# The first batch's last 64 tokens done later for four pairs at once, and q of three pairs loaded in 1 KB runs

## The chip, the cores and the metric

The kernel runs on one core of a Trainium2 chip. The metric is the device time of the whole program in microseconds. The core has a matrix engine (TensorE, "PE" in the profile, with its weight loads as "PEld"), three engines for elementwise work (VectorE "DVE", ScalarE "ACT", GpSimd "POOL"), and a sync engine "SP", which here only issues DMAs. ACT issues DMAs as well.

## The reference

A retention layer without softmax is followed by a SwiGLU feed-forward block. Eight batches, eight heads, 576 tokens, head width 64; then 4608 tokens of width 512 and a hidden width of 1536.

```python
scores = scale * np.matmul(q, k.transpose(0, 1, 3, 2))
gamma = 1.0 - 2.0 ** (-5.0 - np.arange(H, dtype=np.float32))
Dmat = np.where(rel >= 0, gamma[:, None, None] ** rel[None, :, :], 0.0)
ret = scores * Dmat[None, :, :, :]
return np.matmul(ret, v).astype(np.float32)
...
x = np.ascontiguousarray(attn_out.transpose(0, 2, 1, 3)).reshape(B * S, H * D)
...
g = x @ w_gate
silu = g * (1.0 / (1.0 + np.exp(-g)))
val = x @ w_val
return (silu * val @ w_out).astype(np.float32)
```

## The kernel before

Attention works by pairs of heads: pair `i` is batch `i // 4`, heads `2p` and `2p + 1` with `p = i % 4`, and there are 32 pairs. The 576 tokens of a pair are nine chunks of 64. Within a chunk the scores are masked by decay (`near`, with the separate `last_near` for the ninth chunk); what earlier chunks contribute goes through a running 64x64 state for each head. A pair passes through three `tick`s: in tick `i` its q and k are transposed and its k is scaled (`transposes`), in tick `i + 1` come scores, chunk states and masks (`scores`, `new_states`, `masked`), in tick `i + 2` the values and their way into `x` (`own_values`, `earlier_values`, `to_x`). The values of a pair gather in one PSUM tile, `outer`; scores and states use another, `inner`; four more banks, A, B, C and E, belong to the projections and, in the first batch, to the transposes.

The order of the instructions on every engine is written out by hand, and each engine takes its instructions in that order. First come ticks 0 to 5 for the first batch (pairs 0 to 3). During these nothing else can be done, since the feed-forward block needs `x`. The first batch's q and k are loaded token-major and transposed by PE against an identity (L471), copied out of PSUM (L472), and the ninth chunk goes through bankC in the same way (L476, L479). `load(i)` issues the DMAs of pair `i`; in the first batch a row of the load is 64 floats. Batches from the second on are loaded with 32-wide rows and transposed by DVE in 32x32 blocks (L489).

From the moment when the first two pairs are in `x` the up-projection `up0` of the first 512 tokens begins (L772): a 128x512 product for each of 12 hidden blocks `f`, gate and value, into banks A and B for even `f` and C and E for odd. Its weights arrive in DMAs of 256 KB, later of 1 MB (L385, L387), are taken apart by ACT (`split`, L404 and L405) and put together with rounding by DVE (`rounding`, L418 and L419). After the first two `f`, a `plan` is worked off: for each `f` from 2 on the roundings due, `up0(f)`, the next load, and a tick of the second batch: tick 4 after `f=2`, tick 5 after `f=3`, tick 6 after `f=5`. So the PE work of tick 5 (states and scores of pair 4) stands between `f=3` and `f=4`. From 512 tokens on the feed-forward block runs in tiles of 1024 tokens by a fast matrix multiplication scheme with written-out sums (L1003 and L1050), with the remaining ticks spread among the steps.

In the first batch SP's queue holds, in order: the small table, the loads of pairs 0 to 3 (shared with ACT's queue for pairs 0 and 1), the second table, sixteen weight DMAs of 256 KB, load 4, one weight DMA of 1 MB, load 5, load 6 and so on. ACT's queue issues the further 1 MB weight loads as its splits make room. The compiler gives each DMA of these two queues one of eight semaphores, in turn; a DMA waits at its issue until the one that had its semaphore before, eight places earlier, has landed.

Names that the change touches: `CW` is 512 (eight chunks of a pair), `D` and `L` are 64, `NC` is 9, `NFULL` is 4, `HP` is 4, `SQ` is 32; `early[i]` holds the transposed q of pair `i` of the first batch; `even` and `state` hold states; `qry` and `qry_odd` are the decays of the queries with the scale, applied in `to_x` by DVE (L627; L651 for the ninth chunk); `key` those of the keys (L504 on DVE and POOL, L506 on ACT).

Of the kernel before, what the change touches and what calls it, by code (L numbers as in the profile page):

```python
# [22 lines left out]
def tables(gamma, scale, L):  # L23
# [12 lines left out]
    pieces = scale * np.stack(half, axis=2).reshape(2 * L, -1)  # L36
    parts = [twice((g[:, None] ** -at).T), twice((g[:, None] ** (L - at)).T),
             both(g[:, None] ** L), both(g[:, None] ** (2 * L)), pieces, both(scale * g[:, None] ** at),
# [116 lines left out]
def kernel(  # L155
# [32 lines left out]
    nc = tc.nc  # L188
# [65 lines left out]
    io = const.tile([P, 1024], F32, name="io")  # L254

# [8 lines left out]
    def whole(i):  # L264

        return i < needed(2) - 2
# [4 lines left out]
    def load(i):  # L271
# [6 lines left out]
        if i < HP:  # L278
            qk = late[0] if late else ld.tile([P, 2, S // SQ, SQ], F32, tag="qk", name="qk").rearrange("p n j d -> p (n j d)")[:, 0 : NC * D]
            queues = (nc.sync, nc.scalar if i < 2 else nc.sync)  # L280
            for dst, src in ((qk, q), (kn, k)):
                dst = dst.rearrange("p (g d) -> p g d", d=D)
                for n, at in enumerate((slice(0, NFULL + 1), slice(NFULL + 1, NC))):
                    queues[n].dma_start(out=dst[:, n::2], in_=tokens(src, b, p)[:, at])
            queues[i % 2].dma_start(out=t.rearrange("p (g d) -> p g d", d=D), in_=tokens(v, b, p))
# [21 lines left out]
    def chunk(i, hl, c, paired=False):  # L307

        if whole(i):
            g, r = divmod(NC * hl + c, 2)  # L310
            g = 2 * g % NC if paired else g
            return half[r], slice(g * D, (g + 1) * D)
        if c + 1 == NC:
            return half[hl], slice(CW, CW + D)
        return half[c % 2], slice((2 * (c // 2) + hl) * D, (2 * (c // 2) + hl + 1) * D)

    def column(i, hl, c):

        return ts((c - hl) % NC if i < HP else c, L)
# [6 lines left out]
    NCOL = 2 * H + 4 * HP  # L326
# [8 lines left out]
    piece = tab[:, NCOL - 2 * HP : NCOL]  # L335
# [12 lines left out]
    decay(slice(0, H), slice(0, H), half[0])  # L348
    decay(odd_heads, even_heads, half[1])
    decay(even_heads, odd_heads, half[1])  # L350
    nc.gpsimd.tensor_copy(out=last_near, in_=near[:, even_heads])
# [71 lines left out]
    for f in range(2):  # L423
        for m in range(2):
# [8 lines left out]
    spare = rest[:, dn_at + 2560 : sum_at]  # L433
    other = (spare[:, 0:CW].rearrange("p (h c i) -> p h c i", h=2, i=L), spare[:, CW : CW + L],
             spare[:, 640 : 640 + NC * D].rearrange("p (c d) -> p c d", d=D))
    early = [spare[:, 640 + S * (1 + i) : 640 + S * (2 + i)] for i in range(HP)]
# [6 lines left out]
    def last_scores(i):  # L443
        return bankE[:, 0:L] if i < HP else sr
# [14 lines left out]
    def transposes(i):  # L459
# [7 lines left out]
        if i < HP:  # L467

            for t, src, bank in ((kT, kn, bankB), (qT, qk, bankA)) if i else ((qT, qk, bankA), (kT, kn, bankB)):
                for c in range(NFULL):  # L470
                    nc.tensor.transpose(bank[:, ts(c, P)], src[:, ts(c, P)], ident)  # L471
                copy(t[:, 0:CW], bank)  # L472
            tails = ((kT, kn), (qT, qk))
            for n, (_, src) in enumerate(tails):
                for hl in range(2):
                    nc.tensor.matmul(bankC[half[hl], ts(n, L)], src[half[hl], CW : CW + D], ident[half[hl], half[hl]],  # L476
                                     start=True, stop=True, skip_group_check=True)
            for n, (t, _) in enumerate(tails):
                copy(t[:, CW:S], bankC[:, ts(n, L)])  # L479
# [13 lines left out]
        def keys():  # L493
            blocks = kn.rearrange("p (g d) -> p g d", d=D)
            if i < HP:
                parts = [(0, every, blocks[:, 0 : NC - 1 : 2]), (1, every, blocks[:, 1:NC:2]), (1, half[1], blocks[half[1], NC - 1])]
            elif whole(i):
# [38 lines left out]
    def new_states(i):  # L536
        s = st[i]
        for c in range(NFULL):
            for r in range(2):
                for hl in range(2):  # L540
                    rows, at = chunk(i, hl, 2 * c + r)
                    nc.tensor.matmul(z[half[hl], r, c], s["kn"][chunk(i, hl, 2 * c + r, i < HP)], s["v"][rows, at],  # L542
                                     start=True, stop=True, skip_group_check=True)

    def earlier_values(i):
# [6 lines left out]
        for hl in range(2):  # L552
# [3 lines left out]
        for c in (1, 3, 4, 6, 5, 7, 2, 8) if whole(i) else range(1, NC):  # L556
            for hl in range(2):
                nc.tensor.matmul(xr[half[hl]] if c + 1 == NC else value(i, hl, c), state[half[hl], c, :],  # L558
                                 s["qT"][half[hl], column(i, hl, c)], start=False, stop=True, skip_group_check=True)
# [656 lines left out]
```

## Time and profile before

| what | us |
|---|---|
| three runs | 1040.08, 1041.9, 1045.64; median 1041.9 |
| the profiled execution | 1040.84 |
| its span (first to last instruction) | 1039.1 |
| PE busy | 1025.6 |
| PE busy in 0 to 40 us | 32.04 |
| DVE busy in 0 to 40 us | 23.92 |
| ACT busy in 0 to 40 us | 16.14 |
| POOL busy in 0 to 40 us | 7.29 |
| first transpose of pair 0 on PE | 4.29 |
| first up-projection on PE | 26.39 |
| PE work of tick 5 begins | 57.81 |

The profile comes from one execution, recorded by the hardware. A row of the timeline reads: start in us, busy us, engine, line, operation, destination and sources, count, and in brackets how long the engine had been idle and what released it. Consecutive instructions of one kind are put together. "SPq" and "ACTq" rows are DMAs at their issue; the time shown is that of the issue, and not of the transfer. Rows of the waits read: engine and line, what it waited for, us in total, times, the longest. Rows of the windows read: the stretch, its length, busy us of each engine with the number of instructions, the granted clock, the busy share of the DMA engines and GB/s. Matmuls are pipelined and their ends are modelled.

### The profile page before, as it was taken

What the parts mean: (1) busy time and instruction counts of PE and PEld (TensorE: products, weight loads), DVE (VectorE), ACT (ScalarE), POOL (GpSimd) and SP (SyncE); (2) the same over time, 40 slices, a digit from 0 to 9 for tenths busy, and PEclk for the clock granted to TensorE, in tenths of its full rate; (3) what the DMA queues carried; (4) which work ended last, traced back from release to release, by engine and by line L of the source; (5) the groups of instructions that cost most, each with busy time, mean ns of one, the idle gap of its engine ahead of it and who ended that gap; (6) DMA issues with size and microseconds to landing.
All of it is one profiled execution on the core that took longest, in us unless ns stands there. A gap on an engine that the chain in (4) does not pass through costs nothing.

```text
span 1039.1 us, 21528 instructions
## 1 busy us (share of the span) xinstructions
PE 1025.6 (99%) x8448; PEld 843.2 (81%) x8448; DVE 642.3 (62%) x1091; ACT 297.4 (29%) x646; POOL 400.5 (39%) x347
## 2 busy tenths in 40 slices
PE   7999999999999999999999999999999999999998
PEld 6444555888888888888888888888888888888887
DVE  5588868776768767546458785435466644344644
ACT  4475433243544222222322103223211022231110
POOL 2002376766565036522133058212240583222505
PEclk9999999999999999999999999999999999999999
DMA  9999877776679887674676686545554465555653
GB/s 244 251 283 276 190 208 270 195 212 191 195 190 256 213 249 217 186 196 134 186 229 173 176 202 216 152 138 153 158 172 150 143 195 154 152 153 162 180 162 100
DMA packets 310380, 199.10 MB, mean 192 GB/s; under 512 B 220168, under 2 KB 254984, under 8 KB 310280
## 3 DMA queue, kind: packets, MB, share of 16 engines
q1 hardware_dynamic: 279000, 161.51, 57.3%
q10 hardware_dynamic: 31280, 36.22, 10.4%
q8 instruction: 67, 1.10, 0.4%
q14 instruction: 33, 0.27, 0.1%
HBM read 157.56 MB, written 40.11 MB: 190 GB/s over the span
## 4 chain that ended last, share of the span: by engine, by line
PE 78%; DVE 2%; issue 1%; ACT 0%; DVEq 0%
PE bankC L1003 13%; PE bankE L1003 13%; PE bankB L1003 13%; PE bankA L1003 13%; PE bankB L1050 6%; PE bankC L1050 6%; PE bankA L1050 6%; PE bankE L1050 6%; PE outer L531 1%; PE inner L572 1%; PE outer L558 1%; PE inner L542 1%; DVE rest L806 1%; DVE arena L806 0%; DVE rest L940 0%
## 5 line engine op out<-in xcount | busy, mean ns | idle before, releaser
L940 POOL TENSOR_TENSOR rest<-rest 128x512 f32<-128x512 f32 x65 | 91.6, 1414 | 299.1 <-DVE rest L940 279.8
L1024 ACT ACTIVATE io<-rest 128x256 f32<-128x256 f32 x180 | 74.8, 416 | 303.5 <-DVE rest L940 260.8
L1003 PE MATMUL bankC<-rest,arena 128*128 128x256 f32 x544 | 129.1, 380 | 0.0
L1003 PE MATMUL bankA<-rest,arena 128*128 128x256 f32 x544 | 128.7, 379 | 0.0
L806 POOL TENSOR_TENSOR arena<-arena 128x512 f32<-128x512 f32 (+1 forms) x72 | 111.5, 1561 | 36.1 <-DMA up<-arena 23.9
L1003 PE MATMUL bankE<-rest,arena 128*128 128x256 f32 x512 | 121.4, 380 | 0.9 <-DVE rest L940 0.9
L1003 PE MATMUL bankB<-rest,arena 128*128 128x256 f32 x512 | 121.2, 379 | 0.0
L1031 POOL TENSOR_TENSOR arena<-rest,io 128x256 f32<-128x256 f32 x72 | 51.9, 726 | 167.8 <-ACT io L1024 167.8
L1003 PEld LDWEIGHTS bankA<-rest,arena 128*128 128x128 f32 x544 | 103.2, 190 | 14.5 <-issue 0.5
L1003 PEld LDWEIGHTS bankC<-rest,arena 128*128 128x128 f32 x544 | 102.9, 190 | 14.6 <-POOL arena L806 0.3
L1003 PEld LDWEIGHTS bankE<-rest,arena 128*128 128x128 f32 x512 | 96.9, 190 | 14.6 <-DVE rest L940 1.4
L1003 PEld LDWEIGHTS bankB<-rest,arena 128*128 128x128 f32 x512 | 97.1, 190 | 13.3
L806 POOL TENSOR_TENSOR rest<-rest 128x256 f32<-128x256 f32 (+1 forms) x66 | 67.4, 1042 | 95.9 <-DMA qk<-in_k_dram 60.1
L940 DVE TENSOR_TENSOR rest<-bankB,rest 128x512 f32<-128x512 f32 x72 | 48.9, 687 | 67.4 <-PE bankB L1003 51.5
L940 DVE TENSOR_TENSOR rest<-bankC,rest 128x512 f32<-128x512 f32 x72 | 48.9, 687 | 65.8 <-PE bankC L1003 47.1
L940 DVE TENSOR_TENSOR rest<-bankA,rest 128x512 f32<-128x512 f32 x72 | 48.9, 687 | 61.5 <-PE bankA L1003 44.1
L940 DVE TENSOR_TENSOR rest<-bankE,rest 128x512 f32<-128x512 f32 x71 | 48.2, 687 | 60.0 <-PE bankE L1003 46.7
L1027 DVE SCALAR_TENSOR_TENSOR arena<-rest,io 128x256 f32<-128x256 f32 x84 | 58.5, 698 | 11.1 <-ACT io L1024 11.0
L1050 PE MATMUL bankB<-arena 128*128 128x256 f32 x252 | 58.3, 381 | 0.3 <-DVE arena L806 0.3
L1050 PE MATMUL bankA<-arena 128*128 128x256 f32 x252 | 58.0, 380 | 0.2 <-DVE arena L806 0.2
L1050 PE MATMUL bankC<-arena 128*128 128x256 f32 x252 | 58.1, 380 | 0.0
L1050 PE MATMUL bankE<-arena 128*128 128x256 f32 x252 | 57.9, 379 | 0.0
(192 smaller groups left out, 1617.0 us busy)
## 6 DMA issues: line engine op xcount, KB each, us to landing
arena<-up SPq DMA_DIRECT2D x234, 256.0 KB, 2.6
arena<-dn SPq DMA_DIRECT2D x104, 384.0 KB, 3.8
up<-arena ACTq DMA_DIRECT2D x78, 256.0 KB, 4.1
dn<-rest SPq DMA_DIRECT2D x78, 128.0 KB, 1.9
out_dram<-rest SPq DMA_DIRECT2D x31, 256.0 KB, 4.1
qk<-in_q_dram SPq DMA_DIRECT2D x108, 72.0 KB, 2.3
qk<-in_k_dram SPq DMA_DIRECT2D x108, 72.0 KB, 3.3
rest<-in_moe_w_out_dram ACTq DMA_DIRECT2D x6, 1024.0 KB, 5.1
```

Of the source, the lines that this page charges most:

```text
L531: m = nc.tensor.matmul(value(i, hl, c), s["v"][rows, at], ret[rows, c % 2 if whole(i) else hl, c // 2], start=start, stop=start, skip_grou ...
L542: nc.tensor.matmul(z[half[hl], r, c], s["kn"][chunk(i, hl, 2 * c + r, i < HP)], s["v"][rows, at], start=True, stop=True, skip_group_check= ...
L558: nc.tensor.matmul(xr[half[hl]] if c + 1 == NC else value(i, hl, c), state[half[hl], c, :], s["qT"][half[hl], column(i, hl, c)], start=Fal ...
L572: nc.tensor.matmul(sc[chunk(i, hl, 2 * c + r)[0], r if whole(i) else hl, c], kT[half[hl], at], qT[half[hl], at], start=True, stop=True, sk ...
L806: eng.tensor_tensor(out=dst, in0=srcs[0], in1=srcs[1], op=ALU.add if op[0] == "add" else ALU.subtract)
L940: eng.tensor_tensor(out=at(op[1]), in0=at(op[2]), in1=at(op[3]), op=ALU.add if op[0] == "add" else ALU.subtract)
L1003: m = nc.tensor.matmul(b[:, gv * TB : (gv + 1) * TB], w[:, gv, ts(c, P)], rhs[:, c, :], start=(opens and gv == 0 and c == 0), stop=(c == 1 ...
L1024: nc.scalar.activation(out=s, in_=src[:, 0:TB], func=AF.Silu, scale=-1.0 if negative else 1.0)
L1027: return lambda: nc.vector.scalar_tensor_tensor(out=dst, in0=src[:, TB : 2 * TB], scalar=-1.0, in1=s, op0=ALU.mult, op1=ALU.mult)
L1031: nc.gpsimd.tensor_tensor(out=dst, in0=src[:, TB : 2 * TB], in1=s, op=ALU.mult)
L1050: nc.tensor.matmul(b[:, m * TB : (m + 1) * TB], lhs[:, qd, ts(m, P)], w[:, qd], start=(opens and qd == 0 and m == 0), stop=(qd == NQ - 1), ...
```

## The change

In the first batch each pair now stops after eight chunks (512 tokens). Its loads are made head by head, k and v still in rows of 64 floats, and q of pairs 1 to 3 in runs of four tokens (1 KB), into the place that the transposed q takes later. GpSimd reads q from there, puts it into the order that the transposes expect, and multiplies it by the decay of the query and the scale (`scale_run`, with the new table `runs`). For these three pairs `to_x` is then a plain copy on ACT, where it was a product on DVE. ACT's copy of the transposed q writes every fourth column. The tail's transposes, copies, scores, values and products of the first batch are gone from ticks 0 to 5.

The last 64 tokens of all four pairs are done in ticks 5 and 6 of the running order, among the up-projections. `end_loads` issues sixteen loads of q and k (128 partitions in all, rows of 32 floats) and four of v on SP, behind load 5 and ahead of load 6. `end_transposes` is two DVE transposes ahead of tick 5. Tick 5 then has `end_scores` on PE behind pair 4's scores, and `end_masks` on DVE; tick 6 has `end_own` and `end_earlier` on PE and `end_to_x` on DVE. The state ahead of the ninth chunk is kept in `end_states`. The change of the decay mask to the layout of the later batches (`decay`, `last_near`) moves behind the first batch. In the fourth pair's tick the first weight split and the transposes change places with the values of pair 1.

```diff
-        return i < needed(2) - 2
+        return HP <= i < needed(2) - 2
+    def scaled(i):
+        return 0 < i < HP
...
-            for dst, src in ((qk, q), (kn, k)):
-                dst = dst.rearrange("p (g d) -> p g d", d=D)
-                for n, at in enumerate((slice(0, NFULL + 1), slice(NFULL + 1, NC))):
-                    queues[n].dma_start(out=dst[:, n::2], in_=tokens(src, b, p)[:, at])
-            queues[i % 2].dma_start(out=t.rearrange("p (g d) -> p g d", d=D), in_=tokens(v, b, p))
+            for h, queue in zip(heads, queues):
+                if scaled(i):
+                    queue.dma_start(out=early[i][:, ts(h % 2, CW // 2)], in_=q[b, h, 0:CW].rearrange("(p c) d -> p (c d)", c=NFULL))
+                else:
+                    queue.dma_start(out=blocks(qk)[:, h % 2], in_=q[b, h, 0:CW].rearrange("(c p) d -> p c d", p=P))
+            for h, queue in zip(heads, queues):
+                queue.dma_start(out=blocks(kn)[:, h % 2], in_=k[b, h, 0:CW].rearrange("(c p) d -> p c d", p=P))
+            for h in heads:
+                queues[i % 2].dma_start(out=blocks(t)[:, h % 2], in_=v[b, h, 0:CW].rearrange("(c p) d -> p c d", p=P))
...
-                copy(t[:, 0:CW], bank)
-            tails = ((kT, kn), (qT, qk))
-            for n, (_, src) in enumerate(tails):
-                for hl in range(2):
-                    nc.tensor.matmul(bankC[half[hl], ts(n, L)], src[half[hl], CW : CW + D], ident[half[hl], half[hl]],
-                                     start=True, stop=True, skip_group_check=True)
-            for n, (t, _) in enumerate(tails):
-                copy(t[:, CW:S], bankC[:, ts(n, L)])
+                if t is qT and scaled(i):
+                    copy(t[:, 0:CW].rearrange("p (t c) -> p c t", c=NFULL), bank.rearrange("p (c t) -> p c t", c=NFULL))
+                else:
+                    copy(t[:, 0:CW], bank)
...
+                    if scaled(i):
+                        nc.scalar.copy(out=dst(lo, end)[to].rearrange("p (c r i) -> p c r i", r=2, i=L)[:, :, r], in_=xo[src, :, r])
+                        continue
...
+    def end_loads():
+        for n, src in enumerate((q, k)):
+            for a in range(P // SQ):
+                for j in range(2):
+                    nc.sync.dma_start(
+                        out=end_raw[a * SQ : (a + 1) * SQ, n].rearrange("t (n j d) -> t n j d", n=HP, d=SQ)[:, :, j],
+                        in_=src[0, a // 2 : H : 2, CW + j * SQ : CW + (j + 1) * SQ, (a % 2) * SQ : (a % 2 + 1) * SQ].rearrange("n t d -> t n d"))
+        for hl in range(2):
+            for x in range(2):
+                nc.sync.dma_start(out=end_v[half[hl ^ x], 2 * x : 2 * x + 2],
+                                  in_=v[0, 4 * x + hl : 4 * x + 4 : 2, CW:S].rearrange("n t d -> t n d"))
+    def end_transposes():
+        for n, to in enumerate((end_q, end_k)):
+            nc.vector.transpose(out=to.rearrange("p n i -> p (n i)"), in_=end_raw[:, n])
+    def end_scores():
+        for n, x, hl in ends:
+            nc.tensor.matmul(end_at[x][half[hl ^ x], n], end_k[half[hl], 2 * x + n], end_q[half[hl], 2 * x + n],
+                             start=True, stop=True, skip_group_check=True)
...
+    def scale_run(i):
+        if scaled(i):
+            src = early[i].rearrange("p (h c d) -> p h c d", h=2, d=D)
+            dst = loaded[i][0][:, 0:CW].rearrange("p (c h d) -> p h c d", h=2, d=D)
+            table = run[:, 8 * i : 8 * i + 8].rearrange("p (h c) -> p h c", h=2).unsqueeze(3).to_broadcast([P, 2, NFULL, D])
+            nc.gpsimd.tensor_tensor(out=dst, in0=src, in1=table, op=ALU.mult)
...
+            scale_run(t + 1)
             if lo < t < hi:
                 new_pair()
+            if t + 1 == HP:
+                split(0)
             if lo <= t - 2 < hi:
                 own_values(t - 2)
-            for f in transposes(t) if lo <= t < hi else ():
+            for f in transposes(t) if lo <= t < hi and t + 1 < HP else ():
                 f()
-            if t + 1 == HP:
-                split(0)
             if lo <= t - 2 < hi:
                 earlier_values(t - 2)
                 if t == HP:
                     up0(0, range(2))
                 to_x(t - 2)[0]()
+            for f in transposes(t) if t + 1 == HP else ():
+                f()
...
         if lo <= t - 1 < hi:
             scores(t - 1, t - 2 < lo)
+            if t == HP + 1:
+                end_scores()
...
     load(HP + 1)
+    for to, heads in ((even_heads, odd_heads), (odd_heads, even_heads)):
+        decay(heads, to, half[1])
+    nc.gpsimd.tensor_copy(out=last_near, in_=near[:, even_heads])
+    end_loads()
...
         if f in tick_at:
+            if tick_at[f] == HP + 1:
+                plan.append(end_transposes)
             plan.append(lambda t=tick_at[f]: tick(t, HP, FIRST))
```

## The prediction

> **What bounds the kernel now.** First the engine shares of the page, then TensorE's own waits from 36 us on, then busy time by stretch, the timeline of the first 76 us, and the SP queue with its waits.
>
> ```profile
> PE 1025.6 (99%) x8448; PEld 843.2 (81%) x8448; DVE 642.3 (62%) x1091; ACT 297.4 (29%) x646; POOL 400.5 (39%) x347
> ```
> ```profile
> PE bankE L1003 <- DVE rest L940: 0.9, 1, 0.9
> PE bankB L1050 <- DVE arena L806: 0.3, 1, 0.3
> PE bankA L1050 <- DVE arena L806: 0.2, 1, 0.2
> ```
> ```profile
> 0.00:40.00 40.00, 32.04 (x631) 22.76 (x632) 23.92 (x62) 16.14 (x34) 7.29 (x18) 1.00 0.99 254
> 40.00:80.00 40.00, 40.00 (x289) 19.11 (x288) 27.62 (x58) 23.79 (x42) 0.00 (x0) 1.00 1.00 258
> ```
>
> PE is busy 99%, and after 36 us its waits add up to 1.4 us. So only two things count: how much earlier the dense work begins (in the first 40 us PE works 32.04, DMA share 0.99), and whether anything new makes PE wait afterwards. Any such wait is added in full, for no later idle time can absorb it. The front's chain runs over PE and DVE:
>
> ```profile
> 23.54 1.28 DVE L627 TENSOR_TENSOR rest<-outer,tab 128x256 f32<-128x256 f32 x3
> ...
> 24.88 1.01 PE L531 MATMUL outer<-ret,v 64*64 64x64 f32 x32 [1.52 <-DVE rest L627]
> ...
> 28.44 0.19 PEld L772 LDWEIGHTS bankB<-rest,arena 128*128 128x128 f32 x1 [0.24 <-issue]
> ```
>
> Pair 2 waits for DVE to empty the PSUM tile `outer` of pair 1. Now the place where the moved work goes, tick 5: PE first, then DVE, then the two DMA queues.
>
> ```profile
> 57.81 0.69 PE L542 MATMUL inner<-v,kn 64*64 64x64 f32 x32
> ...
> 58.44 0.64 PE L572 MATMUL inner<-qT,kT 64*64 64x64 f32 x30
> ...
> 59.01 3.70 PE L772 MATMUL bankA<-rest,arena 128*128 128x512 f32 x8
> ...
> 59.70 0.69 DVE L777 TENSOR_TENSOR arena<-bankE,io 128x512 f32<-128x512 f32 x1
> ...
> 60.30 0.68 DVE L579 TENSOR_TENSOR ret<-inner,near 128x512 f32<-128x512 f32 x1
> ```
> ```profile
> 51.87 0.45 SPq L298 DMA_DIRECT2D kn<-in_k_dram  x1
> ...
> 59.57 0.39 SPq L298 DMA_DIRECT2D v<-in_v_dram  x1
> ...
> 61.03 0.49 SPq L293 DMA_DIRECT2D qk<-in_q_dram  x1
> ...
> 62.58 1.03 SPq L293 DMA_DIRECT2D qk<-in_q_dram  x1
> ...
> 61.93 0.38 ACTq L385 DMA_DIRECT2D rest<-in_moe_w_gate_dram  x1
> ```
> ```profile
> SPq L298 <- DMA rest<-in_moe_w_out_dram: 7.2, 1, 7.2
> ```
>
> SP stands still 7.2 us before the v of load 5, because the semaphore which that DMA takes over is still held by the 1 MB load of w_out (issued by ACT at 53.16). The built program deals eight DMA semaphores in turn to all DMAs of SP and ACT, and each DMA waits for the one eight places before it. PE reaches the up-projection of f=4 at 59.01.
>
> **What the Trainium skill says.** "DMA: Bandwidth & Descriptors", section "Anatomy of one DMA": the issuing sequencer waits for a semaphore before dispatch, and a DMA has a fixed part of some 2 us, mostly completion. The trace agrees: SP's 7.2 us stand before the issue, and the 128 KB stores to `dn` land after 1.9 us in the median. Same page, "Specifications": runs under 512 B do not reach line rate. The trace agrees: from 2 to 12 us 10053 packets of mostly 256 B move at about 270 GB/s, from 65 to 66 us 377 GB/s in 2 KB packets. "TensorE: Matmul & The Clock Gate", Part 1: after an idle window of about 3.4 us PE runs at half clock until one such window is busy. The trace fits: 64x64 weight loads take 223 ns up to about 17 us and 135 ns later.
>
> **The change, part by part.**
>
> *Front, PE and its copies.* For each of four pairs the eight-chunk form drops the tail transposes (L476: 0.48 + 0.42 us for pair 0), two tail copies (0.22 + 0.21), the third key scaling (0.25 DVE, 0.34 ACT, 0.45 POOL), the score and value matmuls of chunk 8, L589 (0.21) and L651 (0.23). Pair 0's scores then follow the kT copy, at 7.4 instead of 7.9. Pair 1: the two ACT tail copies (0.43) go too, 13.03 becomes about 12.1. Pair 2: 18.55 becomes about 17.3.
>
> *Front, DVE to ACT and POOL.* `to_x` of pairs 1 to 3 becomes three ACT copies. DVE loses 3 x 1.28 us. ACT gains 3 x 1.1 (0.37 for a 128x256 copy from PSUM, row L583), and loses 1.3 of tail copies. GpSimd gains three 128x512 multiplications, 1.41 us each by row L940 POOL (1.56 by row L806), and loses two parts of 0.45. They run at about 7, 10 and 13.5 us, while POOL waits 12.2 us for PE in this trace, so only q1's lies near the path: q1 should land at about 7, be scaled by 8.6, and its transposes come at 10.2. Cover 1.6 us; without it the delay is what exceeds it. The q copy on ACT now writes with a stride of four elements; no row shows it: between 0.58 (as contiguous) and 1.2 us; I take 0.6, as no element more is moved, and it matters three times. With these, `outer` of pair 1 is emptied at about 21.4 instead of 24.82, and bankB of f=0 begins at about 24.7 instead of 28.44. Front gain on PE about 3.5 us (2.5 to 4.5; the transposes of pair 3, put behind the values of pair 1, bare a PE drain of 0.25).
>
> *Front, DMA.* 12 tails of 32 KB go, 1.45 us at 270 GB/s. Three q of 256 KB move in 1 KB runs: at 340 instead of 270 GB/s 0.6 us. The larger first table costs 0.06. So SP's and ACT's loads, which are held by DMA rate from 2 us on, come about 1.9 us earlier (1 to 3).
>
> *The end loads.* SP gets 20 more DMAs (16 of q and k, 16 KB in 128 B runs, then four of v) behind load 5 and ahead of load 6. DVE gets two transposes ahead of tick 5's first mask, and they wait for all 16; PE gets eight score matmuls directly ahead of f=4, and these wait for DVE. Queued behind: all of PE's f=4 to 6, and on DVE mask, states, transposes and roundings. In the built program v of load 5 takes w_out's semaphore as before; the fourth q load takes that of w_val (ACT at 57.36; SP could go on at 62.58 in this trace); the fourth k load that of w_gate (ACT at 61.93; its packets end at about 66.6). With all this 1.9 us earlier:
> - v of load 5 at 57.7; q loads 1 to 3 at 58.1, 58.6, 59.0 (0.45 each: 0.35 for the first table of 128 runs, 0.49 for a q load of 576).
> - q load 4 at 62.58 - 1.9 = 60.7; eight DMAs up to k load 3 end at 64.3.
> - k load 4 at 66.6 - 1.9 = 64.7; k load 8 issued at 66.5, landed 2.2 later (1.9 in the `dn` row, 2.2 the least for L293) at 68.7.
> - DVE's second transpose 0.4 (L489 takes 0.75 for 576 columns, here 256), PE's 16 score instructions 0.3: f=4 begins at 69.5 instead of 59.01.
>
> That is **+10.5 us**, and it already holds the front gain: PE merely arrives earlier, at about 56, and stands for about 13 us. Bounds: 0.37 an issue and loads 3 us earlier give +8; 0.55 and 1 us give +13.
>
> *After the stall.* PE comes back cold. By the skill's window 3.4 to 6.8 us at half clock, loss 1.7 to 3.4; I take 2.5 (an estimate; no restart in this trace shows it). Tick 6 gets 16 value matmuls, 32 instructions at 0.63/32 us (row L558): 0.6. The two masks, three products and two moved decays lie on DVE and POOL beside 13.7 us of f=4 and f=5; DVE starts its mask with PE then, where now it is 1.3 us behind. Load 6 moves behind the end loads, but its use moves as far.
>
> Sum: 10.5 + 2.5 + 0.6 = **+13.6**. On the profiled execution's 1040.84 (span 1039.1 and 1.7 around it) 1054.4; that execution is 1.1 below the median of the three runs, within their spread of 5.6. I predict 1054.5.
>
> **Rivals.**
> - *A shorter stall*: SP isn't held by all three weights, or ACT issues them sooner; the q and k loads land at 60 to 65. For: ACT's issue times hang on splits that start earlier too. Against: w_val is issued at about 55.5 in any case and took 5 us. Stall 2 to 7 us beyond 59, with less of the clock loss: 1043 to 1050. 12%.
> - *Not slower: the end loads are there in time*, and the front gain remains. It decides when the last k load lands before about 55.5. SP would have to issue the 16 loads, 7.2 us, from about 46 on, when it still issues load 5; against it stands the whole 7.2 us wait. 3.5 us gained less 0.9 for the 48 end instructions: 1038.3, and up to 1035 with a larger front gain. 12%.
> - *A longer stall*: each small DMA takes SP about 1 us, as the four q of load 6 did (4.1 us together), 13 x 0.5 more: 1059 to 1066. 8%.
> - *GpSimd's ordering of q is late* and the front gains nothing: the end stall hides that, so the time is the main case's; it is in the 68%.
>
> **How the numbers follow.** Main case 68%: 1050.5 (bounds low: 8 + 1.7 + 0.6) to 1058 (13 + 3.4 + 0.6). Range 1045 to 1060: it leaves out most of the not-slower and longer rivals. 0.5% is 5.2 us, about what a measurement of this kernel can tell. Slower by more than that, above 1047.1: main, longer, and half of the shorter stall, 0.82. Within: 0.14, for most of the not-slower case gains less than 5.2. Faster: 0.04.
>
> **What would show it.** In the changed profile: a gap on PE of 10 us or more ahead of the end scores (L704), put down to DVE; DVE idle ahead of its transposes (L698), put down to a DMA of k; SP issuing L688 from about 58 to 67; PE's first up-projection at about 23 to 24; after the gap slower matmuls for some us. If L704 follows the scores of tick 5 without a gap, the prediction is wrong at its centre; if the gap is there but half as long, in the semaphore waits or the issue time.

## The result, and the profile after

| | kernel before | changed kernel |
|---|---|---|
| median of four runs, us | 1041.49 | 1060.11 |
| lowest and highest, us | 1040.08, 1045.64 | 1057.29, 1062.0 |
| profiled execution, us | 1040.84 | 1058.27 |
| its span, us | 1039.1 | 1056.5 |

The ratio is 1.0165 (95% interval 1.0141 to 1.019): 1.65% slower. The forecast was 1054.5, with a range of 1045 to 1060; the median lies 0.1 above the range. The medians differ by 18.6 us, the spans of the two profiled executions by 17.4; what follows explains the 17.4.

The engines' shares come first, from the page of the changed kernel:

```profile
PE 1025.2 (97%) x8416; PEld 841.9 (80%) x8416; DVE 639.8 (61%) x1078; ACT 299.9 (28%) x648; POOL 403.0 (38%) x349
```

PE is busy as long as before (1025.6 us then), with the slower matmuls after the stall counted in, so nearly the whole loss shows as time in which PE stands. PE's three longest waits from 20 us on (engine, line, what it waited for: us in total, times, longest; "issue" means that the profile shows nothing that PE waited for):

```profile
PE outer L704 <- DVE rest L698: 15.2, 1, 15.2
PE inner L574 <- issue: 1.8, 1, 1.8
PE outer L533 <- ACT rest L641: 0.6, 1, 0.6
```

There is one wait at the end scores, and a second one, of 1.8 us, without a releaser: the profile names nothing that ended it. The timeline of PE shows both in their place:

```profile
55.74 0.64 PE L574 MATMUL inner<-qT,kT 64*64 64x64 f32 x30
71.58 0.71 PE L704 MATMUL outer<-rest 64*64 64x64 f32 x16 [15.21 <-DVE rest L698]
72.22 5.11 PE L846 MATMUL bankA<-rest,arena 128*128 128x512 f32 x8
77.17 3.60 PE L846 MATMUL bankB<-rest,arena 128*128 128x512 f32 x8
...
92.11 0.62 PE L574 MATMUL inner<-qT,kT 64*64 64x64 f32 x25 [1.79 <-issue]
```

What DVE waits for stands in its own rows. It is idle for 9.29 and then for 3.11 us, and each transpose takes only 0.45. The first transpose is that of q (`end_q` in `end_transposes`), so its wait is for the q loads, though the row names a DMA of k; the second is for those of k.

```profile
67.53 0.45 DVE L698 STREAM_TRANSPOSE rest<-rest 128x256 f32<-128x256 f32 x1 [9.29 <-DMA rest<-in_k_dram]
71.08 0.45 DVE L698 STREAM_TRANSPOSE rest<-rest 128x256 f32<-128x256 f32 x1 [3.11 <-DMA rest<-in_k_dram]
```

SP's queue (at its issues), with its three longest waits from 50 to 80 us:

```profile
56.48 0.39 SPq L311 DMA_DIRECT2D v<-in_v_dram  x1
56.96 7.44 SPq L688 DMA_DIRECT2D rest<-in_q_dram  x8
64.51 4.97 SPq L688 DMA_DIRECT2D rest<-in_k_dram  x8
69.59 2.74 SPq L693 DMA_DIRECT2D rest<-in_v_dram  x4
```
```profile
SPq L311 <- DMA rest<-in_moe_w_out_dram: 4.9, 1, 4.9
SPq L688 <- DMA rest<-in_moe_w_val_dram: 3.0, 1, 3.0
SPq L688 <- DMA rest<-in_q_dram: 1.2, 1, 1.2
```

The eight q take 7.44 us, of which 3.0 is the wait for w_val's semaphore, and the eight k 4.97, of which 1.2 is a wait for a q load eight places earlier. The last k is issued at 69.05 and has landed at about 70.9; DVE goes on at 71.08.

The windows after the stall (stretch, length, busy us and instructions of PE, PEld, DVE, ACT and POOL, granted clock, DMA share, GB/s) show how PE comes back:

```profile
72.00:74.00 2.00, 2.00 (x14) 0.94 (x7) 1.53 (x7) 0.00 (x0) 0.00 (x0) 0.50 0.30 60
74.00:76.00 2.00, 2.00 (x5) 0.92 (x4) 2.00 (x5) 0.00 (x0) 0.00 (x0) 0.73 0.81 132
76.00:78.00 2.00, 2.00 (x6) 0.83 (x5) 1.83 (x6) 1.24 (x2) 0.00 (x0) 1.00 0.85 138
```

PE runs at half clock until about 75, and bank A of f=4 takes 4.95 us from its start to that of bank B, where the kernel before took 3.54. A PE at half clock is called cold below.

The sum, from the starts of the same work in both timelines: f=4 begins at 72.22 instead of 59.01 (+13.2); its first bank is 1.4 longer; tick 6 lasts from 87.56 to 92.66 instead of from 72.94 to 75.20 (+2.84: the 1.79 without a releaser, and 1.05 of added matmuls). Together that is +17.46, and it stays so to the end: the last write of bank E by L1077 begins 17.44 us later than its counterpart (L1003). The front did gain: the PE work of tick 5 begins at 55.11 instead of 57.81, 2.7 us earlier, and the first bank E of f=3 accordingly. The stall swallows it.

In the front the rows of ACT and PE say why it is 2.7 and not 3.5:

```profile
11.21 0.58 ACT L483 COPY kT<-bankB 128x512 f32<-128x512 f32 x1 [0.64 <-PE bankB L479]
12.11 1.06 ACT L481 COPY rest<-bankA 128x512 f32<-128x512 f32 x1 [0.31 <-PE bankA L479]
...
21.52 1.12 ACT L641 COPY rest<-outer 128x256 f32<-128x256 f32 x3
```
```profile
13.22 1.13 PE L574 MATMUL inner<-rest,kT 64*64 64x64 f32 x32 [1.20 <-ACT rest L481]
...
22.87 0.69 PE L533 MATMUL outer<-ret,v 64*64 64x64 f32 x32 [0.61 <-ACT rest L641]
```

The copy of the same 128x512 tile takes 0.58 us contiguous and 1.06 with every fourth column written, and PE waits for it. The scores of pair 1 come at 13.22, no earlier than before (13.03). The gain lies at `to_x` of pair 1, now three copies on ACT: pair 2's own values begin at 22.87 instead of 24.88.

### The profile page after: what moved, and what is told of

It reads as the page before. It is cut to its first block, busy times and chain, and to the rows that moved or that the text cites. A ratio compares the mean times of both kernels' runs of the same rounds, so it can differ in the third digit from the quotient of the medians.

```text
span 1056.5 us, 21497 instructions
## 1 busy us (share of the span) xinstructions
PE 1025.2 (97%) x8416; PEld 841.9 (80%) x8416; DVE 639.8 (61%) x1078; ACT 299.9 (28%) x648; POOL 403.0 (38%) x349
## 4 chain that ended last, share of the span: by engine, by line
PE 91%; DMA 4%; DVE 2%; SPq 1%; issue 1%; ACT 1%; POOL 0%; ACTq 0%; DVEq 0%; POOLq 0%
PE bankC L1077 13%; PE bankA L1077 13%; PE bankE L1077 12%; PE bankB L1077 12%; PE bankB L1124 6%; PE bankC L1124 6%; PE bankA L1124 6%; PE bankE L1124 5%; PE outer L533 2%; PE bankA L846 2%; PE inner L574 2%; PE bankB L846 1%; PE outer L560 1%; PE inner L544 1%; PE bankC L846 1%; PE bankE L846 1%
## 5 line engine op out<-in xcount | busy, mean ns | idle before, releaser
L1077 PE MATMUL bankC<-rest,arena 128*128 128x256 f32 x544 | 129.1, 380 | 0.4 <-POOL arena L1048 0.4
L1077 PE MATMUL bankA<-rest,arena 128*128 128x256 f32 x544 | 128.8, 380 | 0.1
L1077 PE MATMUL bankE<-rest,arena 128*128 128x256 f32 x512 | 121.4, 380 | 0.5 <-DVE rest L1014 0.5
L1077 PE MATMUL bankB<-rest,arena 128*128 128x256 f32 x512 | 121.2, 379 | 0.0
L1077 PEld LDWEIGHTS bankA<-rest,arena 128*128 128x128 f32 x544 | 103.1, 190 | 14.9 <-issue 0.9
L1077 PEld LDWEIGHTS bankC<-rest,arena 128*128 128x128 f32 x544 | 102.9, 190 | 15.1 <-POOL arena L1048 0.8
L1077 PEld LDWEIGHTS bankE<-rest,arena 128*128 128x128 f32 x512 | 96.9, 190 | 14.2 <-DVE rest L1014 0.9
L1077 PEld LDWEIGHTS bankB<-rest,arena 128*128 128x128 f32 x512 | 97.1, 190 | 13.3
```

Source lines behind the costliest of these rows:

```text
L1077: m = nc.tensor.matmul(b[:, gv * TB : (gv + 1) * TB], w[:, gv, ts(c, P)], rhs[:, c, :], start=(opens and gv == 0 and c == 0), stop=(c == 1 ...
```

## The experiments

The theory to test (A): the sixteen q and k loads of the end land late, and PE stands for them. Its rivals: the transposes' place in DVE's order would make PE wait anyway (B), or much of the loss has another source (C). Each group of runs had its own runs of the kernel before beside it. Their medians were 1044.1 to 1045.4, and single ones of them lay between 1040 and 1050; so the ratios are read, and from single profiles only waits and starts, not totals. These medians are some 3 to 4 us above the 1041.49 of the first group, near which the times expected for e4, e5, e6 and e1 lie.

| run | median us | ratio (95%) | wait at end scores | PE gap in tick 6 |
|---|---|---|---|---|
| changed kernel | 1060.11 | 1.0165 (1.0141 to 1.019) | 15.2 | 1.8 |
| e4, no q and k loads | 1049.46 (one) | | 2.4 | 0.6 |
| e5, loads first | 1054.26 | 1.0086 (1.0059 to 1.0112) | 3.7 | 4.2 |
| e6, and transposes first | 1051.3 | 1.0064 (1.0051 to 1.0076) | 2.5 | 4.1 |
| e1, one tick later | 1051.62 | 1.0057 (1.0036 to 1.0079) | 4.3 | none |
| e7, e6 with PE's queue shifted | 1050.28 | 1.0068 (1.0043 to 1.0093) | 1.4 | none |
| e9, loads on GpSimd | 1043.67 | 0.9993 (0.998 to 1.0007) | none | none |
| e10, e9 with plain q | 1046.47 | 1.0019 (1.0006 to 1.0032) | none | none |
| e11, e9 with the stride on PE | 1043.14 | 0.9994 (0.9978 to 1.0009) | none | none |
| e12, e11 with a small shift | 1046.41 | 1.0014 (1.0002 to 1.0026) | none | none |
| e13, e11 with no shift | 1049.84 | 1.0055 (1.0039 to 1.0071) | none | 4.9 |
| e14, before with a shift | 1047.61 | 1.0018 (1.0002 to 1.0033) | | none |
| e15, e13 with the end's values apart | 1047.82 | 1.0028 (1.0013 to 1.0044) | none | 1.8, in f=6 |

**Without the loads (e4).**

```diff
     def end_loads():
-        for n, src in enumerate((q, k)):
+        for n, src in enumerate(()):
```

> The 16 loads of q and k of the end are left out, so the last 64 tokens of batch 0 are computed from stale data; all PE, DVE, ACT and GpSimd work of the changed kernel is kept, and the four loads of v. Theory A (the loads land late, and PE stands for them): PE's wait at the end scores falls from 15.2 to 2 to 3 us, which is what the transposes cost by their place behind up0(3)'s product on DVE (they would end at about 59, PE is there at 56.4); time 1041 to 1043.5, some 17 less than the changed kernel. Rival B (DVE's order is the loss, the loads were hidden behind it): wait of 8 us or more stays, time above 1050. Rival C (half of the loss is elsewhere, in the added work of ticks 5 and 6 and a slower front): wait gone, time still 1046 to 1052.

The end is then computed from what lies in the buffers. Its PE waits from 25 us on, and the starts of f=4 and f=6:

```profile
PE outer L704 <- DVE rest L698: 2.4, 1, 2.4
PE outer L560 <- DVE state L609: 1.8, 1, 1.8
PE inner L574 <- issue: 0.6, 1, 0.6
```
```profile
60.43 5.40 PE L846 MATMUL bankA<-rest,arena 128*128 128x512 f32 x8
...
79.81 3.70 PE L846 MATMUL bankA<-rest,arena 128*128 128x512 f32 x8
```

The wait falls from 15.2 to 2.4 us with nothing gone but these loads, and f=4 begins at 60.43 instead of 72.22: A is shown for 11.8 us. (The wait fell by 12.8, but PE also came to it 1.3 us later, at 57.7 instead of 56.4.) The 2.4 are B's share: the transposes stand behind the product of bank E (L851), at 59.22 on DVE. The time, 1049.46 from one execution, is 6 us above A's figure and in C's range, but decides little, for single executions of the kernel before reached 1049.81 in that group. The trace says more: f=6 begins 4.6 us later than in the kernel before (75.20). So C holds for a smaller part: 1.4 us are there at f=4 already, 1.7 are clock loss after the short stall (bank A 5.40 instead of 3.70), and 1.5 are the added work of tick 6 with a PE gap in it. A wait of 1.8 us for DVE comes later.

**The loads ahead of load 5 (e5), and the transposes ahead of up0(3)'s product (e6).**

```diff
+    end_loads()
     load(HP + 1)
...
-    end_loads()
```
```diff
+        if tick_at.get(f) == HP + 1:
+            plan.append(end_transposes)
         plan.append(lambda f=f: up0(f, range(HP)))
...
-            if tick_at[f] == HP + 1:
-                plan.append(end_transposes)
```

> All 20 loads of the end are issued ahead of load 5 instead of behind it; nothing else moves. Theory A: they are issued between about 43 and 53 us and land by 56, so PE's wait at the end scores is the 2 to 3 us of DVE's order; load 5 comes some 8 to 10 us later, which is hidden if its user (tick 5's transposes on DVE) has slack. Time 1041 to 1044. Rival B (order on DVE): wait stays above 8 us, time above 1050. Rival D (the late load takes the place of the late end loads: ACT and DVE stand for pair 5, and f=5 or f=6 waits for its rounding): the wait at the end scores is short, but a new one of 3 to 8 us appears later, time 1045 to 1051.

> As the run before, and the two end transposes stand on DVE ahead of up0(3)'s product instead of behind it. Theory A with the order on DVE as its second part: no wait of PE at the end scores above 1 us, time 1038.5 to 1041, which is the front gain of 2.7 less about 1.5 for the matmuls of the end. If DVE's order costs nothing, the same time as the run before. Rival D: as in the run before, a later wait of 3 to 8 us.

The waits of PE in e5, and then PE in e6:

```profile
PE inner L574 <- issue: 4.2, 1, 4.2
PE outer L704 <- DVE rest L698: 3.7, 1, 3.7
```
```profile
59.10 0.46 PE L704 MATMUL outer<-rest 64*64 64x64 f32 x16 [2.54 <-DVE rest L698]
...
80.53 0.67 PE L574 MATMUL inner<-qT,kT 64*64 64x64 f32 x26 [4.09 <-issue]
81.13 5.40 PE L846 MATMUL bankA<-rest,arena 128*128 128x512 f32 x8
```

The stall falls to 3.7 and 2.5, as A says, and both kernels are faster than the changed one. The times of A (1041 to 1044 and 1038.5 to 1041) were missed by 10 us, of which 3.7 are the slower kernel before in this group. (In e5's profile PE also lost 2.6 us in the front.) In e6 the transposes were still late: roundings stand ahead of them on DVE, and the last k came at 58.6. SP took 7.85 us for the eight k loads, and 4.0 of them were a wait for the semaphore of w_out. The larger part was not foreseen by any theory: in the scores of tick 6 PE now stands for 4.1 us instead of 1.8, for nothing that the profile shows, and then runs cold. Rival D, a wait for load 5, showed on DVE (2.40 and 2.02 us ahead of pair 5's transposes), but no PE wait followed from it.

**The end one tick later (e1).**

```diff
-            if t == HP + 1:
+            if t == HP + 2:
                 end_scores()
```

(The transposes, masks, values and products move by a tick in the same way.)

> The loads stay behind load 5; the end transposes and scores move from tick 5 to 6, values and products from tick 6 to 7. Theory A: the last k lands at about 71, and PE reaches tick 6 at about 73, so the wait is 0 to 2 us; time 1039 to 1042. Load 6 still stands behind the 20 loads on SP, starts at about 70, and may bring a wait of its own at tick 6: then up to 1046. Rival B: the same wait as in the changed kernel, one tick later, time above 1050. Rival C: wait gone, time 1046 to 1052.

PE, then DVE and ACT in e1:

```profile
77.91 0.71 PE L704 MATMUL outer<-rest 64*64 64x64 f32 x16 [4.33 <-DVE rest L698]
78.55 6.39 PE L846 MATMUL bankA<-rest,arena 128*128 128x512 f32 x8
```
```profile
76.49 0.69 DVE L851 TENSOR_TENSOR arena<-bankE,io 128x512 f32<-128x512 f32 x1 [2.33 <-ACT io L850]
77.10 0.76 DVE L698 STREAM_TRANSPOSE rest<-rest 128x256 f32<-128x256 f32 x2
```
```profile
69.50 0.67 ACT L411 ACTIVATE rest<-rest 128x512 f32<-128x512 f32 x1 [3.04 <-DMA rest<-in_q_dram]
...
74.77 0.66 ACT L411 ACTIVATE rest<-rest 128x512 f32<-128x512 f32 x1 [2.39 <-DMA rest<-in_moe_w_out_dram]
```

The loads are there in time (no DMA stands in front of L698), and PE still waits 4.3 us. The last links of the chain are B's: the transposes stand behind L851, L851 waits for ACT's activation, ACT's split for a weight, w_out, that is late. But the first link is the end loads again. ACT issued this w_out at 68.96, after it had stood for the semaphore of an end q load, eight places earlier; the 3.04 us ahead of 69.50 are mostly that stand. So e1 does not separate B from A. The expected 0 to 2 us were wrong because the place in DVE's order was taken as harmless, and because the end loads were counted on SP's queue alone and not among the semaphores that ACT shares.

**The gap without a releaser (e7).** Count in the trace the entries of PE's queue: matmuls and weight loads, two of each for a product in f32, and the rest of its instructions. Then the gap stands behind the same entry, number 1729, in the changed kernel, e4, e5 and e6, though it comes there at four different times. The page has this row of the DMA queues (packets, MB, share of 16 engines), the same before and after:

```profile
q8 instruction: 67, 1.10, 0.4%
```

67 packets of 16 KB, for some 17,200 entries of PE: one packet for about 256. Theory F: PE runs out of instructions at the end of a block. e7 is e6 with 32 products ahead of everything else.

```diff
+    for _ in range(32):
+        nc.tensor.matmul(bankE[half[0], 0:L], ident[half[0], half[0]], ident[half[0], half[0]], start=True, stop=True, skip_group_check=True)
     for t in range(HP + 2):
         tick(t, 0, HP)
```

> The kernel with loads and transposes first (its PE gap in the scores of tick 6 was 4.1 us, after which one bank took 5.40 instead of 3.70 us), plus 32 matmuls of 64x64 whose result nobody reads, put at the start of PE's queue, where PE waits for the first loads. They move every later PE instruction by 64 places (matmul and weight load). Theory F (the gap without a releaser is PE's wait for its own instructions: its queue's 67 fetches of 16 KB hold 256 instructions of 64 B each, tick 6 with the work of the end has some 400 in 3 us, and a fetch asked for at its start came too late): the gap disappears or moves to another place, and with it the slower bank: 5 to 6 us less at f=6, time 1043.5 to 1047 on a chip where the kernel before has 1045. Rival G (the gap belongs to the end's own work, a hidden wait for outer, inner, qT or kT): it stays at 4 us in the same place, time unchanged near 1051.

The bank behind tick 6 in e7:

```profile
77.49 3.70 PE L846 MATMUL bankA<-rest,arena 128*128 128x512 f32 x8
```

No gap, no cold bank: from f=4 to f=6 it takes 17.1 us instead of 21.6 in e6. F's forecast for the place came true. The time did not fall by 5: the 32 products held PE until 8.6 and pushed the front back by more than 2 us (bank A of f=0 at 26.69 instead of 24.4), and waits of 2.6 and 1.5 us appeared at 146 and 202 us in this profile. The unshifted e1 has no gap in tick 6 either: PE stood for DVE there from 73.58 to 77.91, and in that time, at 73.8, the packet began.

**All causes out of the way (e9, e10, e11).** The loads go to GpSimd's queue (`nc.gpsimd.dma_start` in `end_loads`, called behind `last_near`), the transposes ahead of the roundings of f=3, the 32 products stay. e10 sets `scaled` to `False`. e11 moves the stride:

```diff
-                    nc.tensor.transpose(bank[:, ts(c, P)], src[:, ts(c, P)], ident)
-                if t is qT and scaled(i):
-                    copy(t[:, 0:CW].rearrange("p (t c) -> p c t", c=NFULL), bank.rearrange("p (c t) -> p c t", c=NFULL))
-                else:
-                    copy(t[:, 0:CW], bank)
+                    to = bank.rearrange("p (t c) -> p c t", c=NFULL)[:, c] if t is qT and scaled(i) else bank[:, ts(c, P)]
+                    nc.tensor.transpose(to, src[:, ts(c, P)], ident)
+                copy(t[:, 0:CW], bank)
```

> All three causes removed at once: the 20 loads of the end on GpSimd's DMA queue, behind its work in the first batch, so that SP's load 5 comes as before; the end transposes on DVE ahead of the roundings of f=3; the 32 unread matmuls at the start. If the list of causes (late k loads, DVE's order, PE's gap) is whole: no PE wait above 0.7 us at L704 or L574, span that of the kernel before less about 2.7 (front) plus about 1.2 (matmuls of the end): some 1.5 us faster than before, ratio 0.997 to 1.001. Rival H (GpSimd's issue is slow, or its loads take DMA time from load 5 and the weights): a wait of 2 us or more at L698 or at the roundings, ratio 1.002 to 1.008.

> The run before with q of pairs 1 to 3 loaded, transposed and copied plainly and scaled in to_x by DVE, so no 1 KB runs, no multiplications on GpSimd, no strided copy. If the front gain comes from to_x on ACT (as the trace of the changed kernel suggests: own values of pair 2 at 22.87 instead of 24.88), PE's f=0 bankB comes at about 27.5 to 28, 1.2 to 2 us later than with it, and the time is that much more. Rival: the strided copies (1.06 to 1.13 instead of 0.58 us) eat all of it: the same time within 0.7 us.

> The run with the loads on GpSimd, with the stride of four put into the PSUM write of PE's transposes, and ACT's copy of q contiguous. If the stride is what costs ACT 1.06 to 1.13 us, and PE's write bears it: ACT's copy 0.58, pair 1's scores at about 12.7 instead of 13.2, pair 2's at 18.3, bankB of f=0 0.5 us earlier or unmoved, since to_x of pair 1 still ends last there. If the copy was slow for another reason, its time stays at 1.06 to 1.13.

GpSimd's issues in e9, PE at the end scores in e9, and ACT's copy in e11:

```profile
34.34 4.55 POOL L688 DMA_DIRECT2D rest<-in_q_dram  x8
38.88 2.32 POOL L688 DMA_DIRECT2D rest<-in_k_dram  x4
```
```profile
58.69 0.45 PE L704 MATMUL outer<-rest 64*64 64x64 f32 x15
59.06 3.70 PE L846 MATMUL bankA<-rest,arena 128*128 128x512 f32 x8
```
```profile
15.29 0.59 ACT L481 COPY rest<-bankA 128x512 f32<-128x512 f32 x1 [0.31 <-PE bankA L480]
```

e9 is not to be told from the kernel before (0.9993), where the changed kernel was at 1.0165: with late loads, DVE's order and PE's gap out of the way, the loss is gone. The 32 products cost e9 the front gain (bank A of f=0 at 26.98, and 26.39 in the kernel before), so it does not show what the change is worth without them. e11 shows that the stride is what made ACT's copy slow. PE's transposes bear it for nothing (1.06 us for four in e9 and in e11); pair 1's scores come at 15.92 instead of 16.41. That is worth nothing in the total (0.9994 and 0.9993). e10 was a miss in its place: bank B of f=0 came at 28.47, not later than in e9 (28.80). Its time was higher, but its profile has a 1.9 us gap without a releaser at 147 and waits of 0.3 to 0.7 us in tick 5, so what the 1 KB runs with GpSimd's product are worth is not settled.

**Is it the block or the added work (e12, e13, e14, e15)?** e12 has the 32 products with 4 columns and 4 rows (they end at 3.3 us), e13 has none, e14 is the kernel before with 41 of them, and e15 is e13 with `end_own`, `end_earlier` and `end_to_x` behind f=6 instead of in tick 6.

```diff
+        nc.tensor.matmul(bankE[0:4, 0:4], ident[half[0], 0:4], ident[half[0], 0:4], start=True, stop=True, skip_group_check=True)
```
```diff
+        if tick_at.get(f - 1) == HP + 2:
+            plan.append(end_values)
```

> As the run with the loads on GpSimd and the stride on PE, but the 32 unread matmuls take 4 columns and 4 rows instead of 64 and 64, so that they end before the first data is there (they took 7.08 us, from 1.56 to 8.6, and pair 0's transposes came at 8.57 instead of 4.28). Expected: pair 0's transposes at about 4.3 to 4.5, bankB of f=0 at 25.5 to 26.5, tick 5 on PE at about 55 instead of 57.8, no gap in tick 6, time 2 us less than that run: 1040.5 to 1042 where the kernel before has 1044.8, ratio 0.996 to 0.999. Rival: the front gives back what is gained (PE is cold again after the short matmuls): ratio 0.999 to 1.001.

> The run before without the unread matmuls. Theory F (PE waits for its own instructions where a block of 256 begins at the start of tick 6): a gap of 1.5 to 4.1 us on PE in the scores of tick 6, its last instruction again number 1729 of PE's queue, and up to 1.7 us of slow matmuls after it[...]; time 1.5 to 6 us above the run before. If the gap came from the late or crowded loads of the end alone, which are out of the way now, there is none, and the two runs take the same time.

> The kernel before with 41 unread matmuls of 4 columns at the start of PE's queue, nothing else: 164 more entries (matmul and weight load, two passes each), so that a block of 256 entries begins with tick 6 (before, it begins 167 entries into it, at 74.2 us) and ends some 16 entries before the tick does. Theory F: a gap without a releaser of 1 to 4 us near the end of the scores of tick 6 at about 75, in a kernel with none of the end's work; time 1 to 5 us above the kernel before, if the short matmuls cost the front nothing. Rival G (the gap belongs to the end's work): no gap, same time.

> As the run with all causes removed and no unread matmuls (its PE gap in tick 6 was 4.9 us, with 1.1 us of slow matmuls after it), with the end's values and products taken out of tick 6 and put behind f=6, beside no tick. Theory F, with what the shifted kernel before taught (the next block of PE's instructions is asked for 32 to 48 entries before a block ends, so only a run of some 290 to 300 short entries in a row can outrun it; tick 6 with the end's work has 341, without it 275): no gap in tick 6 or behind f=6, one PE drain of 0.2 to 0.3 us between the end's own values and the rest; 5 to 6 us less: median 1044 to 1045.5, ratio 0.9985 to 1.0005. If the gap comes back at the same entry (number 1729, which lies in f=6 now), F in this form is wrong: ratio above 1.003.

PE behind tick 6 in e13, then in e15:

```profile
80.63 1.01 PE L572 MATMUL inner<-qT,kT 64*64 64x64 f32 x26 [4.90 <-issue]
81.57 4.84 PE L844 MATMUL bankA<-rest,arena 128*128 128x512 f32 x8
```
```profile
75.77 3.27 PE L846 MATMUL bankA<-rest,arena 128*128 128x512 f32 x7
80.85 0.59 PE L846 MATMUL bankA<-rest,arena 128*128 128x512 f32 x1 [1.80 <-issue]
```

- e13 has the gap of 4.9 us again, behind entry 1729, with the loads long landed; e12, the same kernel shifted, has none in tick 6. The block shifts the gap, and the loads of the end do not make it. The pair differs by 3.4 us in the median.
- e12's own time missed its mark (1.0014 instead of 0.996 to 0.999): the front was 3 us earlier than in e11 (bank B of f=0 at 25.77 instead of 28.79), and at f=4 nothing was left of it (58.70, and 59.01 in the kernel before). A gap of 1.94 us appeared at 144.8, behind entry 3521.
- e14: no gap in tick 6. F in the form "a block that begins with the tick runs dry" is refuted. The trace shows why: the block in question had been fetched at 64.8, long before tick 6. Number the packets from 0; packet n then brings the entries behind number 449 + 256 n. In all 14 traces none began before PE was within 41 entries of number 193 + 256 n, which is the end of the block two before its own. Counted from 40 entries short of that end, packets began up to 16 us later, 2.2 in the median. My reading was that a tick of 275 short entries does not outrun that and one of 341 can; e15 was to show it.
- e15 shows half of it: the gap falls from 4.9 to 1.8 us, but it is there, again behind entry 1729, in the middle of long up-projections, and by its expectation F in this form is wrong. The length of the run of short entries is not all; the packet's delay matters as much. In e13 and e15 PE was 40 entries short of the mark at 71.2 and 71.7 us, and the packet began at 78.1 and 78.2, some 6.5 to 7 us later; in the changed kernel it was 3.9. What delays a packet is open. The load of the DMA engines does not tell: over 944 packets the delay and the DMA share in the microsecond behind that moment are all but unrelated (correlation 0.08). No run took the weight loads away, which move in that stretch.

The profiles put 15 gaps of PE's matmuls to "issue", of 0.3 us and more, in twelve of the fourteen traces. All stand behind entries 449, 705, 961, 1729, 3521 or 5313: each is 193 and a multiple of 256. One of them is in the kernel before (0.39 us at 27.48). In each of the 15 the packet that brings the next entries began 2.3 to 3.0 us before PE went on: at 89.6 and PE at 92.1 in the changed kernel, 77.9 and 80.5 in e6, 78.1 and 80.6 in e13, 142.2 and 144.8 in e12. So PE waits there for its own instructions.

No version beats the kernel before by more than the measurement can tell. e9, e10 and e11 give the front gain up to the 32 products. e12 and e13 have it, and lose it on the way. In e13 tick 5 is reached 1.9 us earlier, and waits for ACT's key scaling (0.35) and DVE's transposes (0.54), with the end scores, make f=4 begin at 59.04, and 59.01 was the start before. In e11 and e13 the split of the first 1 MB of w_gate begins at 51.1 and 51.2, not at 48.57 as in the changed kernel. That the end's earlier loads take the DMA time of that weight is my reading of it; it was not isolated.

## Why the prediction was right, and where it was off

The mechanism was that of the main case, and the total was longer than its 1050.5 to 1058: the median fell into the band of the rival with the longer stall (1059 to 1066). Term by term, with the front's gain inside the first one, the sum was 13.6 and the trace has 17.46: 2.7 too little for the end loads, 1.1 too much for the clock, 2.2 too little for tick 6.

- **The bound and the place.** "Any such wait is added in full" and "a gap on PE of 10 us or more ahead of the end scores": 15.2 us there, kept to the end as +17.44. e4 shows that the loads make it.
- **The end loads, +10.5.** Mechanism right, the term 2.7 too small. The v of load 5 was issued 1.2 earlier than predicted (56.48), but w_val's semaphore came at 62.1 instead of 60.7, for the step "60.7, all 1.9 us earlier" carried the front's gain over to a transfer that was issued 2.1 earlier and landed only 0.5 earlier. Then came a 1.2 us wait that was not in the sum: k 3 takes over the semaphore of a q load of the same series. The third weight of the sum, w_gate, held nothing. So the last k was there at about 70.9, not 68.7, and f=4 began 1.3 after it instead of 0.8, with the scores at half clock (0.64 instead of 0.3).
- **Cold clock, +2.5.** 1.4 at bank A, at the low bound with the slower scores. The Trainium skill, "TensorE: Matmul & The Clock Gate", Part 1, has PE back at speed after one busy window of about 3.4 us. The windows agree: half clock from 71.58 to about 75. In e1 it took longer, from 77.91 to 84 (bank A 6.39), after a wait of only 4.33. And the idle window of 3.4 us that the prediction took over is no threshold here: after 2.4 us of waiting PE was cold in e4 (bank A 5.40), after 2.5 in e6 it was not.
- **Tick 6, +0.6.** 1.05 of matmuls (0.8 in e9, with the same products and no gap), and 1.8 of a PE gap, which no step had. That step failed by omission: it priced the added instructions by their duration, and not as entries that PE must be given. By e7, e12 and e13 a shift of PE's queue takes the gap out of tick 6.
- **The front, -3.5.** 2.7 at tick 5; the first up-projection came at 24.50, where 23 to 24 was given as the sign. The strided copy was taken at 0.6 ("as no element more is moved"); it takes 1.06 to 1.13, the upper bound. GpSimd's products took 1.04 instead of 1.41 and stayed hidden. DMA: load 4 on SP was reached 1.4 earlier, not 1.9.
- **The rivals.** "End loads there in time, 1038.3" held that the front gain would then remain. In e12 and e13 the loads are there in time and the front is earlier, and the gain does not remain (1.0014 and 1.0055). "A longer stall" was off in its cause (0.62 us a k load, not 1); that its time came true is luck.
- **A reading.** The 10053 packets belong to 0 to 12 us; from 2 to 12 there are 9916, at the 270 GB/s given.

## What to carry to other kernels

When work moves off a front into the dense part, its loads take their place in a queue and among a fixed number of semaphores: count back from each load to the DMA whose semaphore it inherits, the ones of its own series too. Count on from it as well, to the loads of other queues that inherit its semaphore, as w_out on ACT did in e1. And take transfers that are held by the DMA rate as not moving with the front. An operation placed "ahead of the tick" stands behind what waits ahead of it on that engine. And small matmuls are not priced by their microseconds alone where many come in a row: look for gaps without a releaser and count entries.

## What was not expected of the hardware

- PE waits for its own instructions, at fixed places: all 15 gaps stand 256 entries or a multiple of it apart, up to 4.9 us long (e13), and end 2.3 to 3.0 us after a packet of queue q8 begins. The clock was at half for some us afterwards where the gap was long (bank A 5.40 us in e6, 3.70 in e7). What delays a packet is open.
- An ACT copy from PSUM of 128x512 f32 into every fourth column takes 1.06 to 1.13 us, 0.58 contiguous; PE's transposes write PSUM with that stride in the time that they take anyway.
- Twenty small loads went out on GpSimd's queue at about 0.57 us each while that engine was idle, beside SP's queue and without its semaphore waits for weights (e9).
